# Transposing K as fp32 words, two bf16 tiles per TensorE transpose, in a one-token attention kernel

## The chip, the cores and the metric

The kernel runs on one NeuronCore of a Trainium2 chip. The metric is the device time of one execution in microseconds. Comparisons are always against runs of the kernel before, on the same chip and in the same rounds.

## The reference, cut to what matters

One token attends to a cache of 32768 keys and values. There are 32 query heads and 8 K/V heads of 128 dims, so four query heads share one K/V head.

```python
q = (x @ wq).reshape(B, Sq, Hq, Dh)            # Hq = 32, Dh = 128, Sq = 1
scores = einsum("bhqd,bhkd->bhqk", q, k) * Dh**-0.5   # 8 K/V heads, Sk = 32768
p = softmax(scores); o = einsum("bhqk,bhkd->bhqd", p, v)
a = o.reshape(...) @ wo                         # [4096] @ [4096, 512]
out = g * a + (1 - g) * swiglu(x)               # g: a scalar gate
```

K and V are 67 MB each in bf16, the weights 14 MB. Everything is read once: 148.1 MB.

## The kernel before

Loads go through a ring of five slots of 4 MB. One half of a K head (16384 keys) or of a V head fills one slot; the order is K, V, K, V, and the output weights `wo` come last. The sync engine issues a load when the slot's last reader has signalled.

A matmul contracts over partitions, so K (keys on partitions) has to be transposed before the scores. TensorE does this eight tiles at a time into a PSUM bank, and VectorE (DVE) copies the bank to SBUF as `ktT`. Then come eight score matmuls. One half of a head is 16 such groups, and its V half is 128 more matmuls.

```python
def emit_fill(j, src, q):                       # TPF = 8 tiles of 128 keys
    if j >= NST: pe.wait_ge(sem_cp, j - NST + 1)
    stb = pst[j % NST]                          # a PSUM bank seen as bf16
    for t in range(TPF):
        ins = pe.transpose(stb[:, t*128:(t+1)*128], src[:, q*TPF + t, :], ident[:, :])
    ins.then_inc(sem_fill, 1)

def emit_scores(j):                             # 128 keys x 4 heads each
    ...
    pe.wait_ge(sem_cp, j + 1)
    for t in range(TPF):
        col = (q*TPF + t) * HPG                 # HPG = 4
        ins = pe.matmul(ps_sc[f % NSC][:, col:col+HPG],
                        ktT[:, j % NKT, t*128:(t+1)*128],
                        qT[:, g*HPG:(g+1)*HPG], start=True, stop=True)
    ins.then_inc(sem_sc, 1)

# DVE, once per group:
dve.tensor_copy(ktT[:, j % NKT, :], pst[j % NST]).then_inc(sem_cp, 1)   # 128x1024 bf16

# V: src[:, r, :] is the weight, four columns of exp(scores) stream
ins = pe.matmul(ps_o[:, g*HPG:(g+1)*HPG], src[:, r, :], ET[:, g % NEG, :, k], ...)

# sync engine, the last load, in four pieces (WO_CUT = 16, 8, 4, 4 of 32 rows):
sp.dma_start(wo_v[:, j0:j0+n, :], src[:, j0:j0+n, :]).then_inc(sem_ldo[c], 16)
```

Of the kernel before, what the change touches and what calls it, by code (L numbers as in the profile page):

```python
# [6 lines left out]
ALU = mybir.AluOpType  # L7
AX = mybir.AxisListType
BF16 = mybir.dt.bfloat16
FP32 = mybir.dt.float32  # L10
# [3 lines left out]
def bass_gated_mix__gqa_block_cached__swiglu_ffn__decode_kernel(  # L14
# [14 lines left out]
    G = A_k_cache.shape[1]  # L29
    S = A_k_cache.shape[2]  # L30
    DH = A_k_cache.shape[3]
    H = A_wq.shape[1] // DH
    HPG = H // G
# [15 lines left out]
    TPF = 8  # L49
# [3 lines left out]
    NKT = 8  # L53
    NST = 3
    NSC = 3
# [15 lines left out]
    with ExitStack() as es:  # L71

        def S_(name):
            return es.enter_context(nc.semaphore(name))

        def T(name, shape, dt):
            return es.enter_context(nc.sbuf_tensor(name, shape, dt))
# [8 lines left out]
        sem_ident = S_("s_ident")  # L86
        sem_iota = S_("s_iota")
# [17 lines left out]
        sem_prod = S_("s_prod")  # L105
        sem_gpart = S_("s_gpart")
        sem_qT = S_("s_qT")
        sem_t1 = S_("s_t1")
        sem_tT = S_("s_tT")
        sem_omg = S_("s_omg")  # L110
# [15 lines left out]
        ktT = T("ktT", [128, NKT, TPF * 128], BF16)  # L126
        ET = T("ET", [128, NEG, HPG, NT], BF16)
        ident = T("ident", [128, 128], BF16)
        ones_f = T("ones_f", [128, 128], FP32)
        colidx = T("colidx", [128, 128], FP32)  # L130
        kf = T("kf", [128, 1], FP32)
# [11 lines left out]
        g_col = T("g_col", [128, 1], FP32)  # L143
        omg = T("omg", [128, 1], FP32)
        qT = T("qT", [128, H], BF16)
        sg = T("sg", [128, FC], FP32)
        t1 = T("t1", [128, FC], FP32)
        tT = T("tT", [128, FC], BF16)
# [12 lines left out]
        row = T("row", [OC, 128], BF16)  # L161

        ps = es.enter_context(nc.psum_tensor("ps", [128, 8, 512], FP32))
        pst = [ps[:, i, :].bitcast(BF16) for i in range(NST)]
        ps_e = ps[:, 0, :]
        ps_sc = [ps[:, NST + i, :] for i in range(NSC)]
        ps_o = ps[:, 6, :]
        ps_m = ps[:, 7, :]
# [1 line left out]
        ps_r = ps[:, OC, :]  # L170
        M_X0 = 0
        M_Q0 = M_X0 + 2 * KC
        M_G0 = M_Q0 + H
        M_U0 = M_G0 + FC
        M_B0 = M_U0 + FC
        M_O0 = M_B0 + OC
# [5 lines left out]
        def kv_slot(entry):  # L182
            return slot_of(entry).rearrange("p (r d) -> p r d", r=RH)
# [14 lines left out]
        def load_sem(entry):  # L198
            return sem_ld[place[entry]]

        with nc.Block("main") as block:  # L201

            @block.gpsimd
            def _(pool):
                npool = [0]

                def chain(ins):
                    ins.then_inc(sem_pool, 1)
                    npool[0] += 1
                    pool.wait_ge(sem_pool, npool[0])  # L210

                pool.memset(ones_bf[:, :], 1.0).then_inc(sem_ones, 1)
                pool.memset(ones_f[:, :], 1.0).then_inc(sem_ones, 1)
                chain(pool.memset(ident[:, :], 0.0))
                pool.affine_select(
                    out=ident[:, :],
                    in_=ident[:, :],
                    compare_op=ALU.not_equal,
                    fill=1.0,
                    base=0,  # L220
                    pattern=[[-1, 128]],
                    channel_multiplier=1,
                ).then_inc(sem_ident, 1)
                pool.iota(
                    colidx[:, :],
                    pattern=[[1, 128]],
                    base=0,
                    channel_multiplier=0,
                    allow_small_or_imprecise_dtypes=True,
                ).then_inc(sem_iota, 1)  # L230
                pool.iota(
                    kf[:, :],
                    pattern=[[1, 1]],
                    base=0,
                    channel_multiplier=1,
                    allow_small_or_imprecise_dtypes=True,
                ).then_inc(sem_iota, 1)
                for g in range(G):
                    pool.wait_ge(sem_pmax, 3 * (g + 1))
                    pool.partition_all_reduce(  # L240
                        gmax[:, g, :], pmax[:, g, :], 128, ReduceOp.max
                    ).then_inc(sem_gmax, 1)
# [51 lines left out]
            def _(pe):  # L294
# [19 lines left out]
                def emit_q():  # L314
                    pe.wait_ge(load_sem(("wq",)), 16)
                    for h in range(H):
                        for c in range(KC):
                            ins = pe.matmul(  # L318
                                ps_m[:, M_Q0 + h : M_Q0 + h + 1],
                                wq_v[:, c, h * DH : (h + 1) * DH],  # L320
                                xT[:, c : c + 1],
                                start=(c == 0),
                                stop=(c == KC - 1),
                            )
                    ins.then_inc(sem_pe_q, 1)

                def emit_ffn():
                    pe.wait_ge(load_sem(("F1",)), 32)
                    for base, wt in ((M_G0, wg), (M_U0, wu)):
                        for j in range(FC):  # L330
                            for c in range(KC):
                                ins = pe.matmul(  # L332
                                    ps_m[:, base + j : base + j + 1],
                                    wt[:, c, :].rearrange("d (p j) -> d j p", j=FC)[:, j, :],
                                    xT[:, c : c + 1],
                                    start=(c == 0),
                                    stop=(c == KC - 1),
                                )
                    ins.then_inc(sem_pe_h, 1)
# [15 lines left out]
                def emit_fill(j, src, q):  # L355
                    if j >= NST:
                        pe.wait_ge(sem_cp, j - NST + 1)
                    stb = pst[j % NST]
                    for t in range(TPF):
                        ins = pe.transpose(  # L360
                            stb[:, t * 128 : (t + 1) * 128], src[:, q * TPF + t, :], ident[:, :]
                        )
                    ins.then_inc(sem_fill, 1)

                def emit_scores(j):
                    f, q = j // FPH, j % FPH
                    g = f // 2
                    if j == 0:
                        pe.wait_ge(sem_qT, 1)
                    if q == 0 and f >= NSC:  # L370
                        pe.wait_ge(sem_exp, HPG * (f - NSC + 1))
                    pe.wait_ge(sem_cp, j + 1)
                    for t in range(TPF):
                        col = (q * TPF + t) * HPG
                        ins = pe.matmul(  # L375
                            ps_sc[f % NSC][:, col : col + HPG],
                            ktT[:, j % NKT, t * 128 : (t + 1) * 128],
                            qT[:, g * HPG : (g + 1) * HPG],
                            start=True,
                            stop=True,  # L380
                        )
                    ins.then_inc(sem_sc, 1)

                def emit_pv(g, hf, src, r0, n):
# [11 lines left out]

                emit_x()
                pe.wait_ge(sem_xT, 1)
                pe.wait_ge(sem_ident, 1)
                scored = 0  # L400
                filled = 0
                for e in stream[:-1]:
# [15 lines left out]
                    _, g, hf = e  # L418
                    src = kv_slot(e)
                    pe.wait_ge(sem_exp, 2 * HPG * g + HPG * (hf + 1))  # L420
                    if e == ("V", G - 1, 1):
# [5 lines left out]
                            start=True,  # L427
                            stop=True,
# [23 lines left out]
                for c, n in enumerate(WO_CUT):  # L452
                    pe.wait_ge(sem_ldo[c], 16)
                    for j in range(j0, j0 + n):
                        for oc in range(OC):
                            ins = pe.matmul(  # L456
                                ps_a[:, oc, :],
                                wo_v[:, j, oc * 128 : (oc + 1) * 128],
                                O2[:, j : j + 1],
                                start=(j == 0),  # L460
                                stop=(j == WOJ - 1),
                            )
# [8 lines left out]
            def _(act):  # L471
# [6 lines left out]
                act.wait_ge(sem_pe_h, 1)  # L478
                act.activation(sg[:, :], ps_m[:, M_G0 : M_G0 + FC], ACT.Sigmoid).then_inc(
                    sem_sg, 1  # L480
# [23 lines left out]
            def _(dve):  # L504
                ndc = [0]

                def dchain(ins):
                    ins.then_inc(sem_dchain, 1)
                    ndc[0] += 1
                    dve.wait_ge(sem_dchain, ndc[0])  # L510
# [9 lines left out]
                dve.tensor_reduce(gpart[:, :], prod_col[:, :], AX.X, ALU.add).then_inc(  # L520
                    sem_gpart, 1
                )
                dve.wait_ge(sem_iota, 2)
                for i, thr in enumerate((32.0, 64.0, 96.0)):
                    dchain(dve.tensor_scalar(kq[:, i : i + 1], kf[:, :], thr, None, op0=ALU.is_ge))
                dchain(dve.tensor_tensor(kq[:, 3:4], kq[:, 0:1], kq[:, 1:2], ALU.add))
# [11 lines left out]
                )  # L538
                dve.tensor_copy(pmat[:, :], pmat_f[:, :]).then_inc(sem_pm, 1)
                dve.wait_ge(sem_pe_q, 1)  # L540
                dve.tensor_copy(qT[:, :], ps_m[:, M_Q0 : M_Q0 + H]).then_inc(sem_qT, 1)
                dve.wait_ge(sem_g, 1)
                dve.tensor_scalar(
                    omg[:, :], g_col[:, :], -1.0, 1.0, op0=ALU.mult, op1=ALU.add
# [2 lines left out]
                def emit_t():  # L547
                    dve.wait_ge(sem_sg, 1)
                    dve.tensor_tensor(
                        t1[:, :], sg[:, :], ps_m[:, M_G0 : M_G0 + FC], ALU.mult  # L550
                    ).then_inc(sem_t1, 1)
# [91 lines left out]
```

## Time and profile before

The median was 362.18 us of 3 runs (362.18 to 362.22).

| what | value | view |
|---|---|---|
| span of the profiled run | 360.6 us | page |
| DMA busy, mean rate | 90% or more in nearly all slices, 413 GB/s | page |
| PE, DVE busy | 79%, 52% | page |
| one K half and one V half at the stream's rate | 19.4 us | stretches |
| one group of 8 transposes and 8 scores, warm | 0.65 us | timeline |

The page of the kernel before: busy time by engine, the clock granted to TensorE and the DMA's share in 40 slices (in tenths), the DMA queues, the chain that ended last, and the costliest groups. PE stands for TensorE's matmuls, PEld for its weight loads, DVE for VectorE, ACT for ScalarE and POOL for GpSimd. A group's line gives the source line, engine, operation, output and inputs, shapes and count, then its busy time in us and the mean ns of one, and last the idle time before it with what ended most of it. "issue" is idle time for which the profile shows no releaser.

```profile
PE 283.3 (79%) x6582; PEld 277.6 (77%) x6582; DVE 187.4 (52%) x305; ACT 27.8 (8%) x140; POOL 4.2 (1%) x18
...
PEclk9999678676879696778788796867895885857655
DMA  8999999999999999999999999999999999999972
...
q1 hardware_dynamic: 6200, 148.12, 96.4%
q8 instruction: 51, 0.84, 0.9%
...
PE 66%; issue 25%; DMA 6%; DVE 1%; ACT 0%; POOLq 0%; SPq 0%; POOL 0%; ACTq 0%; DVEq 0%
...
L360 PE MATMUL ps<-ident,ring 128*128 128x128 bf16 x2048 | 187.9, 252 | 21.2 <-issue 13.7
L360 PEld LDWEIGHTS ps<-ident,ring 128*128 128x128 bf16 x2048 | 150.3, 114 | 24.5 <-issue 16.2
L375 PE MATMUL ps<-qT,ktT 128*128 128x4 bf16 x2048 | 90.9, 166 | 9.1 <-issue 7.9
```

Two readings compete here. The DMA line says that the stream never rests. The chain says that the PE is what everything waited for. Two more views separate them. The first is the table by stretches of 19.4 us, where the columns are the length, the busy time of each engine, the granted clock, the DMA share and the rate:

```profile
160.00:179.40 19.40, 15.61 (x364) 15.40 (x362) 11.52 (x18) 3.10 (x17) 0.37 (x1) 0.76 1.01 430
179.40:198.80 19.40, 14.87 (x371) 14.63 (x368) 11.22 (x17) 0.00 (x0) 0.00 (x0) 0.85 1.01 429
```

In each pair of K and V halves the PE is not busy for about 4 us, and the DMA is never idle. The second is the timeline in the middle of a K half (start, length, engine, instruction). "PE L360 x8" starts at 184.52 and again 0.65 us later: that is one group.

```profile
184.52 0.61 PE L360 MATMUL ps<-ident,ring 128*128 128x128 bf16 x8
184.97 0.34 PE L375 MATMUL ps<-qT,ktT 128*128 128x4 bf16 x8
185.17 0.61 PE L360 MATMUL ps<-ident,ring 128*128 128x128 bf16 x8
```

The lengths include the pipeline's latency. What a group costs is read from start to start: 0.445 us from the first transpose to the first score, and 0.20 us for the eight scores. This is 56 ns per transpose and 25 ns per score.

The PE's waits in the kernel before (total, number, longest) mostly have no releaser that the profile shows, hence "issue":

```profile
PE ps L387 <- issue: 29.6, 15, 3.2
PE ps L360 <- issue: 13.7, 11, 2.1
...
PE ps L375 <- issue: 7.9, 10, 1.2
...
PE ps L360 <- DMA ring<-in_A_k_cache_dram: 7.4, 1, 7.4
```

### The profile page before, as it was taken

The numbers are of one execution on the slowest core, as the hardware profiler recorded it, in microseconds if no ns is written. First come the engines' busy times: TensorE is split into PE (matmuls) and PEld (weight loads), VectorE is DVE, ScalarE is ACT, GpSimd is POOL, SyncE is SP. The second block draws the span as 40 slices with busy tenths as digits, with TensorE's granted clock in tenths as the row PEclk, the third lists the DMA queues.
The fourth block names the chain that finished last, engine by engine and source line by source line (L and its number), as shares of the span: only waits on it lengthen the run. The fifth ranks groups of instructions, "written<-read, shape, count | busy, mean of one in ns | idle before, by whom it ended". The sixth has DMA issues, their size and how long they took to land.

```text
span 360.6 us, 14008 instructions
## 1 busy us (share of the span) xinstructions
PE 283.3 (79%) x6582; PEld 277.6 (77%) x6582; DVE 187.4 (52%) x305; ACT 27.8 (8%) x140; POOL 4.2 (1%) x18
## 2 busy tenths in 40 slices
PE   0439998869796897988786969889879778879674
PEld 0439997869696886988685969889779778879674
DVE  0219186637566383737384664638364744728201
ACT  1000004000110003000300012000300030000300
POOL 0000000000000000000000000000000000000000
PEclk9999678676879696778788796867895885857655
DMA  8999999999999999999999999999999999999972
GB/s 346 411 405 449 420 423 448 413 431 433 416 447 416 431 430 427 420 433 427 428 436 409 448 413 434 433 413 453 407 434 432 418 434 429 427 431 412 411 314 88
DMA packets 6260, 148.99 MB, mean 413 GB/s; under 512 B 698, under 2 KB 700, under 8 KB 1212
## 3 DMA queue, kind: packets, MB, share of 16 engines
q1 hardware_dynamic: 6200, 148.12, 96.4%
q8 instruction: 51, 0.84, 0.9%
q14 instruction: 5, 0.04, 0.0%
q10 hardware_dynamic: 4, 0.00, 0.0%
HBM read 148.11 MB, written 0.00 MB: 411 GB/s over the span
## 4 chain that ended last, share of the span: by engine, by line
PE 66%; issue 25%; DMA 6%; DVE 1%; ACT 0%; POOLq 0%; SPq 0%; POOL 0%; ACTq 0%; DVEq 0%
PE ps L360 38%; PE ps L387 13%; PE ps L375 12%; DMA ring<-in_A_k_cache_dram 6%; PE ps L332 2%; PE ps L456 1%; ACT ET L494 0%; DVE ktT L579 0%; PE ps L346 0%; DVE pmaxf L567 0%; PE ps L423 0%; POOLq L201 0%; SPq L250 0%; POOL gmax L240 0%; PE ps L466 0%
## 5 line engine op out<-in xcount | busy, mean ns | idle before, releaser
L579 DVE COPY ktT<-ps 128x1024 bf16<-128x1024 bf16 x256 | 170.7, 692 | 124.0 <-PE ps L360 123.1
L360 PE MATMUL ps<-ident,ring 128*128 128x128 bf16 x2048 | 187.9, 252 | 21.2 <-issue 13.7
L360 PEld LDWEIGHTS ps<-ident,ring 128*128 128x128 bf16 x2048 | 150.3, 114 | 24.5 <-issue 16.2
L375 PE MATMUL ps<-qT,ktT 128*128 128x4 bf16 x2048 | 90.9, 166 | 9.1 <-issue 7.9
L375 PEld LDWEIGHTS ps<-qT,ktT 128*128 128x128 bf16 x2048 | 81.5, 99 | 9.4 <-issue 8.0
L387 PE MATMUL ps<-ET,ring 128*128 128x4 bf16 x2048 | 64.9, 168 | 30.0 <-issue 29.6
L387 PEld LDWEIGHTS ps<-ET,ring 128*128 128x128 bf16 x2048 | 59.8, 101 | 31.3 <-issue 30.8
L494 ACT ACTIVATE ET<-ps,nbias 128x128 bf16<-128x128 f32 x64 | 22.5, 376 | 0.2
L484 ACT ACTIVATE nbias<-gmax 128x4 f32<-128x4 f32 x8 | 1.6, 206 | 270.3 <-POOL gmax L240 270.3
L567 DVE TENSOR_REDUCE pmaxf<-ps 128x4 f32<-128x512 f32 x16 | 11.1, 692 | 12.5 <-PE ps L375 12.5
L494 ACT ACTIVATION_READ_ACCUMULATOR ET<-ps,nbias 128x1 f32 x64 | 13.8, 216 | 0.0
L332 PE MATMUL ps<-xT,ring 128*128 128x1 bf16 x112 | 6.9, 198 | 0.0
L332 PEld LDWEIGHTS ps<-xT,ring 128*128 128x128 bf16 x112 | 6.8, 158 | 0.0
L240 POOL PARTITION_ALL_REDUCE gmax<-pmax x8 | 3.0, 373 | 321.8 <-DVE pmax L571 321.8
L301 PE MATMUL ps<-ones_bf,x_row 1*128 1x1 bf16 x4 | 0.3, 172 | 7.9 <-DMA gw_row<-in_gate_w_dram 7.9
L318 PE MATMUL ps<-xT,ring 128*128 128x1 bf16 x128 | 3.6, 165 | 3.6 <-DMA ring<-in_A_wq_dram 3.6
L318 PEld LDWEIGHTS ps<-xT,ring 128*128 128x128 bf16 x128 | 3.5, 104 | 3.6 <-issue 3.6
L301 PEld LDWEIGHTS ps<-ones_bf,x_row 1*128 1x128 bf16 x4 | 0.2, 114 | 7.9 <-DMA gw_row<-in_gate_w_dram 7.9
L456 PE MATMUL ps<-O,ring 128*128 128x1 bf16 x128 | 3.9, 165 | 1.8 <-issue 1.5
L456 PEld LDWEIGHTS ps<-O,ring 128*128 128x128 bf16 x128 | 3.6, 104 | 2.0 <-issue 1.6
L513 DVE CAST xT<-ps 128x4 bf16<-128x4 f32 x1 | 0.2, 161 | 8.4 <-PE ps L301 8.4
L605 DVE SCALAR_TENSOR_TENSOR res<-ps,g_col,b_pre 128x4 bf16<-128x4 f32 x1 | 0.2, 221 | 5.6 <-PE ps L456 5.6
(48 smaller groups left out, 16.5 us busy)
## 6 DMA issues: line engine op xcount, KB each, us to landing
ring<-in_A_k_cache_dram SPq DMA_DIRECT2D x16, 4096.0 KB, 36.9
ring<-in_A_v_cache_dram SPq DMA_DIRECT2D x15, 4096.0 KB, 33.2
ring<-in_A_wq_dram SPq DMA_DIRECT2D x1, 4096.0 KB, 12.4
ring<-in_A_v_cache_dram SPq DMA_DIRECT2D x1, 2048.0 KB, 27.9
ring<-in_A_wo_dram SPq DMA_DIRECT2D x1, 2048.0 KB, 33.7
ring<-in_B_w_gate_dram SPq DMA_DIRECT2D x1, 1792.0 KB, 26.8
ring<-in_B_w_up_dram SPq DMA_DIRECT2D x1, 1792.0 KB, 30.6
ring<-in_B_w_down_dram SPq DMA_DIRECT2D x1, 1792.0 KB, 43.5
```

What stands on the lines that cost most here:

```text
L240: pool.partition_all_reduce(gmax[:, g, :], pmax[:, g, :], 128, ReduceOp.max).then_inc(sem_gmax, 1)
L301: ins = pe.matmul(ps_m[:, base + c : base + c + 1], srcv[:, c, :], ones_bf[0:1, 0:1], start=True, stop=True,)
L318: ins = pe.matmul(ps_m[:, M_Q0 + h : M_Q0 + h + 1], wq_v[:, c, h * DH : (h + 1) * DH], xT[:, c : c + 1], start=(c == 0), stop=(c == KC - 1),)
L332: ins = pe.matmul(ps_m[:, base + j : base + j + 1], wt[:, c, :].rearrange("d (p j) -> d j p", j=FC)[:, j, :], xT[:, c : c + 1], start=(c = ...
L360: ins = pe.transpose(stb[:, t * 128 : (t + 1) * 128], src[:, q * TPF + t, :], ident[:, :])
L375: ins = pe.matmul(ps_sc[f % NSC][:, col : col + HPG], ktT[:, j % NKT, t * 128 : (t + 1) * 128], qT[:, g * HPG : (g + 1) * HPG], start=True ...
L387: ins = pe.matmul(ps_o[:, g * HPG : (g + 1) * HPG], src[:, r, :], ET[:, g % NEG, :, k], start=(k == 0), stop=(k == NT - 1),)
L456: ins = pe.matmul(ps_a[:, oc, :], wo_v[:, j, oc * 128 : (oc + 1) * 128], O2[:, j : j + 1], start=(j == 0), stop=(j == WOJ - 1),)
L484: act.activation(nbias[:, g, :], gmax[:, g, :], ACT.Copy, scale=-SCALE).then_inc(sem_nbias, 1)
L494: act.activation(ET[:, g % NEG, h, hf * RH : (hf + 1) * RH], sc[:, h, :], ACT.Exp, bias=nbias[:, g, h : h + 1], scale=SCALE, accum_out=esu ...
L567: dve.tensor_reduce(pmaxf[:, f, :], sc, AX.X, ALU.max).then_inc(sem_pmax, 1)
L579: dve.tensor_copy(ktT[:, j % NKT, :], pst[j % NST]).then_inc(sem_cp, 1)
```

## The change

Two neighbouring bf16 tiles of K are, per key, 256 values in a row. Read as fp32 they are 128 words of two values. One fp32 transpose moves the words, so partition k of the result holds dims 2k and 2k+1 of a pair of tiles: the first tile on partitions 0 to 63, the second on 64 to 127. The transposes are halved. The scores must then take the even and the odd dims in two accumulating passes, with weights at a stride of two elements, and with q spread over a block-diagonal operand (`qz`) of two times four columns, one block for each tile. The intent was to relieve the PE.

```diff
     def emit_fill(j, src, q):
-        stb = pst[j % NST]
-        for t in range(TPF):
+        stb = pst_f[j % NST]
+        for t in range(0, TPF, 2):
+            two = src[:, q * TPF + t : q * TPF + t + 2, :].rearrange("p r d -> p (r d)")
             ins = pe.transpose(
-                stb[:, t * 128 : (t + 1) * 128], src[:, q * TPF + t, :], ident[:, :]
+                stb[:, t * 64 : (t + 2) * 64], two.bitcast(FP32), ident_f[:, :]
             )
     ...
-        for t in range(TPF):
+        for t in range(0, TPF, 2):
             col = (q * TPF + t) * HPG
-            ins = pe.matmul(ps_sc[f % NSC][:, col : col + HPG],
-                ktT[:, j % NKT, t * 128 : (t + 1) * 128],
-                qT[:, g * HPG : (g + 1) * HPG], start=True, stop=True)
+            kt = ktT[:, j % NKT, t * 128 : (t + 2) * 128].rearrange("p (k e) -> p e k", e=2)
+            for e in range(2):
+                ins = pe.matmul(ps_sc[f % NSC][:, col : col + 2 * HPG],
+                    kt[:, e, :], qz[:, g, e, :], start=(e == 0), stop=(e == 1))
     ...   # cut: masks sel, an fp32 identity, two q matmuls through sel, four copies into qz
```

The DVE copy is untouched: it moves the same 128x1024 bf16 bits.

More of the change, by code (lines that the diff above doesn't have):

```diff
@@ L107, in bass_gated_mix__gqa_block_cached__swiglu_ffn__decode_kernel @@
         sem_qT = S_("s_qT")
+        sem_sel = S_("s_sel")
+        sem_qz0 = S_("s_qz0")
+        sem_pe_qe = S_("s_pe_qe")
+        sem_qz = S_("s_qz")
         sem_t1 = S_("s_t1")
@@ L145, in bass_gated_mix__gqa_block_cached__swiglu_ffn__decode_kernel @@
         qT = T("qT", [128, H], BF16)
+        ident_f = T("ident_f", [128, 128], FP32)
+        evenidx = T("evenidx", [128, 128], FP32)
+        kf1 = T("kf1", [128, 1], FP32)
+        sel = T("sel", [128, 2, 128], BF16)
+        qz = T("qz", [128, G, 2, 2 * HPG], BF16)
         sg = T("sg", [128, FC], FP32)
@@ L163, in bass_gated_mix__gqa_block_cached__swiglu_ffn__decode_kernel @@
         ps = es.enter_context(nc.psum_tensor("ps", [128, 8, 512], FP32))
+        pst_f = [ps[:, i, :] for i in range(NST)]
         pst = [ps[:, i, :].bitcast(BF16) for i in range(NST)]
@@ L172, in bass_gated_mix__gqa_block_cached__swiglu_ffn__decode_kernel @@
         M_Q0 = M_X0 + 2 * KC
-        M_G0 = M_Q0 + H
+        M_QE = M_Q0 + H
+        M_G0 = M_QE + 2 * H
         M_U0 = M_G0 + FC
@@ L223, in _ @@
                 ).then_inc(sem_ident, 1)
+                chain(pool.memset(ident_f[:, :], 0.0))
+                pool.affine_select(
+                    out=ident_f[:, :],
+                    in_=ident_f[:, :],
+                    compare_op=ALU.not_equal,
+                    fill=1.0,
+                    base=0,
+                    pattern=[[-1, 128]],
+                    channel_multiplier=1,
+                ).then_inc(sem_ident, 1)
+                pool.iota(
+                    evenidx[:, :],
+                    pattern=[[0, 2], [2, 64]],
+                    base=0,
+                    channel_multiplier=0,
+                    allow_small_or_imprecise_dtypes=True,
+                ).then_inc(sem_iota, 1)
+                pool.memset(qz[:, :, :, :], 0.0).then_inc(sem_qz0, 1)
                 pool.iota(
@@ L325, in emit_q @@
                     ins.then_inc(sem_pe_q, 1)
+                    pe.wait_ge(sem_sel, 2)
+                    pe.wait_ge(sem_qT, 1)
+                    for e in range(2):
+                        ins = pe.matmul(
+                            ps_m[:, M_QE + e * H : M_QE + (e + 1) * H],
+                            sel[:, e, :],
+                            qT[:, :],
+                            start=True,
+                            stop=True,
+                        )
+                    ins.then_inc(sem_pe_qe, 1)
                 def emit_ffn():
@@ L357, in emit_fill @@
                         pe.wait_ge(sem_cp, j - NST + 1)
-                    stb = pst[j % NST]
-                    for t in range(TPF):
+                    stb = pst_f[j % NST]
+                    for t in range(0, TPF, 2):
+                        two = src[:, q * TPF + t : q * TPF + t + 2, :].rearrange(
+                            "p r d -> p (r d)"
+                        )
                         ins = pe.transpose(
-                            stb[:, t * 128 : (t + 1) * 128], src[:, q * TPF + t, :], ident[:, :]
+                            stb[:, t * 64 : (t + 2) * 64], two.bitcast(FP32), ident_f[:, :]
                         )
@@ L368, in emit_scores @@
                     if j == 0:
-                        pe.wait_ge(sem_qT, 1)
+                        pe.wait_ge(sem_qz, 4)
                     if q == 0 and f >= NSC:
@@ L372, in emit_scores @@
                     pe.wait_ge(sem_cp, j + 1)
-                    for t in range(TPF):
+                    for t in range(0, TPF, 2):
                         col = (q * TPF + t) * HPG
-                        ins = pe.matmul(
-                            ps_sc[f % NSC][:, col : col + HPG],
-                            ktT[:, j % NKT, t * 128 : (t + 1) * 128],
-                            qT[:, g * HPG : (g + 1) * HPG],
-                            start=True,
-                            stop=True,
-                        )
+                        kt = ktT[:, j % NKT, t * 128 : (t + 2) * 128].rearrange(
+                            "p (k e) -> p e k", e=2
+                        )
+                        for e in range(2):
+                            ins = pe.matmul(
+                                ps_sc[f % NSC][:, col : col + 2 * HPG],
+                                kt[:, e, :],
+                                qz[:, g, e, :],
+                                start=(e == 0),
+                                stop=(e == 1),
+                            )
                     ins.then_inc(sem_sc, 1)
@@ L398, in _ @@
                 pe.wait_ge(sem_xT, 1)
-                pe.wait_ge(sem_ident, 1)
+                pe.wait_ge(sem_ident, 2)
                 scored = 0
@@ L522, in _ @@
                 )
-                dve.wait_ge(sem_iota, 2)
+                dve.wait_ge(sem_iota, 3)
                 for i, thr in enumerate((32.0, 64.0, 96.0)):
@@ L540, in _ @@
                 dve.wait_ge(sem_pe_q, 1)
-                dve.tensor_copy(qT[:, :], ps_m[:, M_Q0 : M_Q0 + H]).then_inc(sem_qT, 1)
+                dchain(dve.tensor_scalar(kf1[:, :], kf[:, :], -1.0, None, op0=ALU.add))
+                for e, k in ((0, kf), (1, kf1)):
+                    dve.tensor_scalar(
+                        sel[:, e, :], evenidx[:, :], k[:, 0:1], None, op0=ALU.is_equal
+                    ).then_inc(sem_sel, 1)
+                dve.tensor_copy(qT[:, :], ps_m[:, M_Q0 : M_Q0 + H]).then_inc(sem_qT, 1)
+                dve.wait_ge(sem_pe_qe, 1)
+                dve.wait_ge(sem_qz0, 1)
+                for e in range(2):
+                    qe = ps_m[:, M_QE + e * H : M_QE + (e + 1) * H].rearrange(
+                        "p (g h) -> p g h", g=G
+                    )
+                    for b in range(2):
+                        dve.tensor_copy(
+                            qz[b * 64 : (b + 1) * 64, :, e, b * HPG : (b + 1) * HPG],
+                            qe[b * 64 : (b + 1) * 64, :, :],
+                        ).then_inc(sem_qz, 1)
                 dve.wait_ge(sem_g, 1)
```

## The prediction

> **What bounds the kernel now.** The DMA queue. The page's slices show it 90% busy or more up to the last two; the table by stretches gives DMA share 1.00 to 1.01 and 425 to 430 GB/s in five consecutive 19.4 us stretches (160 to 257 us), each one K half plus one V half (8.39 MB). The queue's own waits (189 us for transposes to free a K slot, 72 us for a V slot) don't starve it: 33 to 37 us from issue to landing means about four transfers queued. 148.1 MB at 428 GB/s is 346 us; startup and a tail of about 7 us after the last bytes (354 to 360.6) make the span. The chain of waits says PE 66%, issue 25%, but that is the consumer following the stream: per 19.4 us pair the PE is busy 15 to 17 us.
>
> **What the PE needs per pair (timeline).** Eight bf16 transposes take 0.47 us (58 ns each, clock 1.00), eight scores 0.20 us (25 ns each); the group repeats every 0.65 us, which is also the pace of the DVE copies (six in 3.93 us). Sixteen groups are 10.4 us, 128 PV matmuls 3.4 us, gaps named issue 2 to 4 us: 16 to 18 of 19.4 us.
>
> **What the change does.**
> - Halves the transposes to 1024. The built program has one load and one matmul per fp32 transpose, so PE instructions fall by about 15%.
> - Makes each load slower. The Trainium skill ("TensorE: Matmul & The Clock Gate", Weight-path perf modes) says Fast Weight Load is off for fp32. The trace agrees in direction: the row sum's fp32 loads took 311 ns at clock 0.50, a bf16 load about 104. Less a fixed 77 ns (104 minus the 27 ns pace), an fp32 load occupies about 230 ns cold, so 115 ns warm, or half that if transpose mode loads in one pass. Estimate: 55 to 115 ns per fp32 transpose warm, 0.22 to 0.46 us per group against 0.47.
> - Scores stay 2048 matmuls, with eight columns instead of four and weights at a stride of two elements. The strided gate/up weights (14 elements) took 61 ns each, the contiguous q projection 28; at stride two I expect 25 to 35 ns.
> - DVE copies are unchanged: 128x1024 bf16, 692 ns.
> - Startup: masks, two q matmuls and four small copies add about 2 us near 17 to 19 us; the PE waits for K until 24.2 us, so this is hidden.
>
> **On the critical path.** Nearly nothing. The group stays near the DVE's 0.65 us, the pair below 19.4 us, and DMA still sets the time. Less instruction fetch may be worth 0.3 us.
>
> **Prediction: 363 us, range 358 to 392.** Faster by over 2%: 4%; within 2%: 66%; slower by over 2%: 30%.
>
> **What would show each step right.** DMA share near 1.00 in the middle; fp32 transposes pacing at most 115 ns; scores near 25 ns; DVE copies at 0.65 us or a little longer; lower PE busy time.
>
> **What would make it wrong.** (1) The fp32 load is not hidden behind the previous matmul, or takes over 160 ns: the group passes 0.9 us and the pair 19.4 us. (2) The transposes stream half as many columns, so the clock falls to 0.50 in the K phase as it does in the PV phase; with 230 ns loads the group is 1.1 us, the pair 23 us, the time over 400 us. (3) The stride of two halves the speed of the score loads. Any of these makes the PE the bound: DMA share below 0.95, longer queue waits for K slots. Faster by over 2% would need a higher DMA rate, which nothing here provides.

## The result, and the profile after

The changed kernel's median was 361.27 us of 4 runs (361.06 to 361.48), against 362.18 us. The ratio is 0.9975, with a 95% interval of 0.9958 to 0.9992. Ratios here are the mean time of one kernel's fast runs over that of the other's in the same rounds, so not quite the ratio of the medians. A second measurement later gave 0.9968 (0.9946 to 0.9991). The gain is small but real: 0.9 us.

The page of the changed kernel, the same parts as before:

```profile
PE 280.0 (78%) x5560; PEld 273.2 (76%) x5560; DVE 192.2 (54%) x312; ACT 27.8 (8%) x140; POOL 4.9 (1%) x22
...
PEclk9999678969596776959587967869595877879555
DMA  8999999999999999999999999999999999999982
...
q1 hardware_dynamic: 6200, 148.12, 96.6%
q8 instruction: 43, 0.70, 0.8%
...
DMA 63%; PE 32%; SPq 2%; issue 1%; DVE 1%; DVEq 0%
...
L403 PE MATMUL ps<-ident_f,ring 128*128 128x128 f32 x1024 | 184.8, 322 | 40.0 <-DMA ring<-in_A_k_cache_dram 40.0
L403 PEld LDWEIGHTS ps<-ident_f,ring 128*128 128x128 f32 x1024 | 136.2, 165 | 41.3 <-DMA ring<-in_A_k_cache_dram 41.3
...
L422 PE MATMUL ps<-qz,ktT 128*128 128x8 bf16 x2048 | 88.6, 167 | 0.4 <-DVE ktT L642 0.4
```

There are half as many transposes, yet their busy time is nearly the same (184.8 against 187.9 us). In the stretches the DMA's share and rate are as before:

```profile
160.00:179.40 19.40, 15.84 (x319) 15.51 (x318) 11.25 (x18) 3.11 (x17) 0.37 (x1) 0.76 1.00 429
179.40:198.80 19.40, 16.94 (x322) 16.54 (x322) 11.68 (x18) 0.00 (x0) 0.00 (x0) 0.76 1.01 430
```

And so does the group in the timeline: four fp32 transposes take 0.473 us from start to first score (118 ns each), and eight scores again 0.20 us. The group is 0.675 us, 4% longer than before.

```profile
186.62 0.63 PE L403 MATMUL ps<-ident_f,ring 128*128 128x128 f32 x4
187.09 0.34 PE L422 MATMUL ps<-qz,ktT 128*128 128x8 bf16 x8
187.29 0.64 PE L403 MATMUL ps<-ident_f,ring 128*128 128x128 f32 x4
```

One view did change a lot. The PE's waits now name the loads, and little is left under "issue":

```profile
PE ps L403 <- DMA ring<-in_A_k_cache_dram: 40.0, 14, 5.9
PE ps L434 <- issue: 10.8, 8, 1.9
...
PE ps L434 <- DMA ring<-in_A_v_cache_dram: 6.3, 5, 3.8
PE ps L503 <- DMA ring<-in_A_wo_dram: 5.0, 4, 3.6
```

The PE now stands at the head of the stream and waits for it. Before, it ran a few microseconds behind and never waited for a load after the first one. Two questions were therefore put to the chip. Why did half the transposes not make the PE's work smaller? And where do 0.9 us come from if the stream carries the same data?

### The profile page after: what moved, and what is told of

Read it like the earlier page. It is cut to its first block, busy times and chain, and to the rows that moved or that the text cites. A ratio compares the mean times of both kernels' runs of the same rounds, so it can differ in the third digit from the quotient of the medians.

```text
span 359.1 us, 11978 instructions
## 1 busy us (share of the span) xinstructions
PE 280.0 (78%) x5560; PEld 273.2 (76%) x5560; DVE 192.2 (54%) x312; ACT 27.8 (8%) x140; POOL 4.9 (1%) x22
## 4 chain that ended last, share of the span: by engine, by line
DMA 63%; PE 32%; SPq 2%; issue 1%; DVE 1%; DVEq 0%
DMA ring<-in_A_k_cache_dram 53%; PE ps L403 19%; DMA ring<-in_A_wo_dram 10%; PE ps L422 6%; PE ps L434 5%; PE ps L372 2%; SPq L297 2%; DVE ktT L642 0%; PE ps L386 0%; PE ps L503 0%; SPq L279 0%; PE ps L513 0%; DVE row L677 0%; DVE res L668 0%; DVEq L667 0%
## 5 line engine op out<-in xcount | busy, mean ns | idle before, releaser
L642 DVE COPY ktT<-ps 128x1024 bf16<-128x1024 bf16 x256 | 174.1, 692 | 111.9 <-PE ps L403 111.3
L403 PE MATMUL ps<-ident_f,ring 128*128 128x128 f32 x1024 | 184.8, 322 | 40.0 <-DMA ring<-in_A_k_cache_dram 40.0
L403 PEld LDWEIGHTS ps<-ident_f,ring 128*128 128x128 f32 x1024 | 136.2, 165 | 41.3 <-DMA ring<-in_A_k_cache_dram 41.3
L422 PEld LDWEIGHTS ps<-qz,ktT 128*128 128x128 bf16 x2048 | 87.5, 98 | 4.0 <-DVE ktT L642 0.6
L422 PE MATMUL ps<-qz,ktT 128*128 128x8 bf16 x2048 | 88.6, 167 | 0.4 <-DVE ktT L642 0.4
L434 PE MATMUL ps<-ET,ring 128*128 128x4 bf16 x2048 | 64.7, 168 | 17.1 <-issue 10.8
L630 DVE TENSOR_REDUCE pmaxf<-ps 128x4 f32<-128x512 f32 x16 | 11.1, 691 | 11.1 <-PE ps L422 11.1
L541 ACT ACTIVATION_READ_ACCUMULATOR ET<-ps,nbias 128x1 f32 x64 | 13.8, 216 | 0.0
```

What stands on the lines that cost most here:

```text
L403: ins = pe.transpose(stb[:, t * 64 : (t + 2) * 64], two.bitcast(FP32), ident_f[:, :])
L422: ins = pe.matmul(ps_sc[f % NSC][:, col : col + 2 * HPG], kt[:, e, :], qz[:, g, e, :], start=(e == 0), stop=(e == 1),)
L434: ins = pe.matmul(ps_o[:, g * HPG : (g + 1) * HPG], src[:, r, :], ET[:, g % NEG, :, k], start=(k == 0), stop=(k == NT - 1),)
L541: act.activation(ET[:, g % NEG, h, hf * RH : (hf + 1) * RH], sc[:, h, :], ACT.Exp, bias=nbias[:, g, h : h + 1], scale=SCALE, accum_out=esu ...
L630: dve.tensor_reduce(pmaxf[:, f, :], sc, AX.X, ALU.max).then_inc(sem_pmax, 1)
```

## The experiments

A caution first. Several of these kernels compute with stale or incomplete K and V on purpose, and all of them still passed the comparison with the reference. The averaged attention term is evidently too small against the tolerance to show it. So the comparison says nothing about whether the fp32 words arrive bit for bit. What supports that here is only the structure of the change, not a run.

### 1 and 2: take the stream away

From the eleventh ring entry on, each load brings 4 of 128 rows, with the same semaphores. This was done to both kernels.

```diff
+                        elif i >= 2 * NSLOT:
+                            sp.dma_start(dst[:, 0:4, :], src[:, 0:4, :]).then_inc(sem_ld[i], 16)
                         else:
                             sp.dma_start(dst, src).then_inc(sem_ld[i], 16)
```

> The kernel before, but from the eleventh ring entry on each K or V load brings only 4 of its 128 rows per partition (wrong result on purpose), so the stream ends after about 90 us and PE and DVE set the rest. Theory A (the DMA stream bounds the whole kernel, PE and DVE have slack): well under 362 us, about 265 us (90 us of stream, then 11 K halves at 10.4 us and 14 V halves at 3.4 us, and the tail). Rival B (the PE chain bounds the kernel, as the chain of waits with 66% PE suggests): within 5% of 362 us.

> The same cut of the loads in the changed kernel. Theory A with equal transposing cost (one fp32 transpose of 117 ns stands for two bf16 of 58 ns): the same as the run before it within 3%, about 268 us, since the group is 0.675 us against 0.647. Rival C (the change made the K phase cheaper and the DMA stream hides the gain): at least 5% faster than the run before it.

Measured: 304.43 us (ratio 0.8399, 0.8369 to 0.8429) for the kernel before, and 306.59 us (0.8462, 0.8449 to 0.8474) for the changed one. So 58 us go when the stream is taken away. That alone does not settle what bounds the kernel, because most of the PE's gaps without a releaser go with the stream (see below). Run 8 settles it: with 1024 matmuls fewer the kernel before gains 1.3 us, and its PE waits 65.6 us for K loads instead. The expected 265 us was wrong. A pair of halves was summed as 13.8 us. The traces show 15.6 us in the kernel before (the long batches of V matmuls start at 159.15 and 221.48 us, four pairs apart) and 15.8 us in the changed one. The first groups of each K half run at half clock, since the clock falls within the V phase (in run 1 it is 0.83 from 159.2 to 162 us, in a V phase, 0.50 from 162 to 164 and 0.95 from 164 to 168). Without the stream, the margin of the PE against 19.4 us is thus about 4 us, not 6.

The changed kernel is 0.7% *slower* without the stream. So no gain was hidden behind it: rival C falls.

"Issue" in the PE's waits also falls from 52.7 us in the kernel before (four groups) to 10.0 us here:

```profile
PE ps L377 <- issue: 3.6, 4, 1.3
PE ps L389 <- issue: 3.2, 2, 3.0
PE ps L362 <- issue: 3.2, 2, 1.7
```

These gaps belong to a loaded DMA. They fall between matmuls that wait for nothing, in the middle of a batch. The instructions themselves are fetched through the same DMA engines (the row "q8 instruction" on the page), and the packed traces show that the gaps are waits for them: in the kernel before there are 36 such gaps over 0.3 us, 52.5 us in all, and every one ends 1.2 to 1.6 us after a block of instructions has landed. So do the eight in the changed kernel (10.8 us) and the seven of run 1, none of which lies between 93 and 278 us, where the stream is cut. With them the PE before had almost no reserve under the stream, although its own work left 4 us. The change did not make that work smaller, but it has fewer instructions to wait for, which is the likely reason that its PE caught up.

### 3 and 4: take the DVE copy away as well

```diff
-                    dve.tensor_copy(ktT[:, j % NKT, :], pst[j % NST]).then_inc(sem_cp, 1)
+                    w = TPF * 128 if j < NKT else 256
+                    dve.tensor_copy(ktT[:, j % NKT, 0:w], pst[j % NST][:, 0:w]).then_inc(sem_cp, 1)
```

> As the first run, and the DVE copies only 256 of 1024 columns from the ninth copy on (wrong result on purpose), so that the PE alone paces the K phase. If the PE paced the group of 0.65 us already: the same as the first run within 2%. If the DVE copy paced it: faster, and the group below 0.62 us.

> The same in the changed kernel. Equal cost: within 3% of the third run, four fp32 transposes in about 0.47 us and eight scores in 0.20 us. Rival C (gain hidden by the DVE copy's pace): group near 0.43 us, about 38 us less than the third run.

Measured: 303.70 us and 306.51 us, so no change in either kernel. The DVE busy time fell from 185.1 to 94.4 us in the kernel before, and the group stayed. The DVE copy only looked as if it set the pace: it runs at the pace at which the PE fills banks.

### 5: load or stream?

An fp32 transpose of 118 ns could be slow because its weights (the K words) load without the fast path, or because 128 fp32 columns of the identity stream slowly. This run builds on the fourth. It loads 32 of the 128 word columns and streams the same identity.

```diff
+                        w = 128 if j < NST else 32
                         ins = pe.transpose(
-                            stb[:, t * 64 : (t + 2) * 64], two.bitcast(FP32), ident_f[:, :]
+                            stb[0:w, t * 64 : (t + 2) * 64], two.bitcast(FP32)[:, 0:w], ident_f[:, :]
                         )
```

> The changed kernel with PE alone (short loads, short DVE copies), and from the fourth fill on each fp32 transpose loads only 32 of its 128 word columns and still streams the 128 columns of the identity (wrong result on purpose). If the fp32 transpose is paced by streaming 128 fp32 columns at two cycles each: still 117 ns each warm, the group 0.675 us, and about 306 us. If it is paced by loading 128 fp32 columns without the fast load: near 55 ns each, the group about 0.45 us, and about 265 us.

Measured: 299.79 us of 2 runs. The timeline gives the pace:

```profile
181.99 0.60 PE L406 MATMUL ps<-ident_f,ring 128*32 128x128 f32 x4
182.42 0.34 PE L427 MATMUL ps<-qz,ktT 128*128 128x8 bf16 x8
182.62 0.60 PE L406 MATMUL ps<-ident_f,ring 128*32 128x128 f32 x4
```

Four transposes take 0.435 us, or 109 ns each, with a quarter of the load. The load did get shorter (the shortest load record fell from 137 ns in run 4 to 92), yet it costs only the last 9 ns of 118. The rest does not depend on the width of the load. By elimination it is the stream: about twice the 56 ns of a bf16 transpose, for the same 128 columns. No run here shortened the stream itself, so this step is argued and not shown. On this reading each fp32 column takes twice the time, and the change moves the same bytes at the same rate.

### 6 to 9: where 0.9 us come from

Theory F is that fewer instruction bytes pass through the DMA engines. Theory L is that the PE no longer lags at the end. Run 6 is the changed kernel again. Run 7 adds 7000 one-element fills on the idle POOL engine. Runs 8 and 9 leave out every other V matmul, in the kernel before and in the changed one.

```diff
# run 7, POOL, after each group's reduction:
+                    for n in range(1000 if g < G - 1 else 0):
+                        pool.memset(junk[:, 1000 * g + n : 1000 * g + n + 1], 0.0)
# runs 8 and 9:
-                    for r in range(r0, r0 + n):
+                    for r in range(r0 + 1, r0 + n, 2):
```

> The changed kernel, unaltered, for comparison on the same chip: 0.9975 of the kernel before, 361.3 us.

> The changed kernel with 7000 one-element fills added on the idle POOL engine, which nothing waits for: 0.45 MB more of instructions to fetch. Theory F (the 0.9 us gain comes from fewer instruction bytes through the same DMA engines; 0.14 MB at 430 GB/s is 0.33 us): 1.0 to 1.3 us slower than the changed kernel. Theory L (the gain comes from the PE no longer lagging behind the stream at the end): no change within 0.3 us.

> The kernel before with every other PV matmul left out (wrong result on purpose): 1024 matmuls and as many loads less on the PE, 0.13 MB of instructions less, 1.7 us of PE time less per pair. Theory L: the PE catches up with the stream and the time falls to that of the changed kernel, about 361.3 us or a little below. Theory F: 0.3 us less than before, 361.8 us. If the PE were the bound: 16 pairs at 1.7 us less, about 335 us.

> The changed kernel with every other PV matmul left out (wrong result on purpose). Theory L: no change within 0.2 us of the changed kernel, since its PE waits for the stream already. Theory F: 0.3 us less. If the PE were the bound: about 335 us.

Measured: 361.34, 390.80, 360.93 and 359.57 us, with 362.23 us for the kernel before (ratios 0.9968, 1.0775, 0.9959 and 0.9920, each to within 0.3%).

Neither theory had the size right. Run 7 lost 29.5 us where bytes over rate give 1.0. Run 9 gained 1.8 us although its PE waits for the stream already, which contradicts theory L, and although its 0.13 MB less is worth only 0.3 us by theory F.

The page of run 7 shows how. The two lines are the rate in each of its 40 slices (9.7 us each) and the queue that fetched for POOL:

```profile
GB/s 324 431 414 435 444 425 423 426 429 426 429 429 422 426 428 429 426 426 426 425 428 426 428 426 429 429 428 412 426 396 399 432 399 432 319 428 204 60 29 17
...
q14 instruction: 60, 0.49, 0.3%
```

At the end the rate is 29 and 17 GB/s. All sixteen engines together move 427, so one moves 27. One DMA engine works on alone, after the others have finished.

The trace can show this for every run. A full-width load raises its semaphore sixteen times, and the trace has the time of each. Below are the sixteen landings of the last piece of `wo`, sorted, in us from the first instruction, in the profiled run of each kernel. They are read from the trace's record of semaphore increments, so this is not one of the profile's printed views.

```
                 eight earlier                                    eight later
before     346.2 346.3 346.4 346.5 347.6 347.9 348.5 352.0 | 355.4 355.4 355.5 355.6 355.7 355.8 357.0 357.3
changed    346.3 346.4 346.4 346.5 347.0 347.3 347.9 351.0 | 353.9 353.9 354.0 354.4 354.4 354.8 355.8 355.8
run 8      346.1 346.2 346.3 346.4 347.5 348.0 348.2 351.9 | 354.2 354.2 354.3 354.4 354.5 354.5 355.5 355.9
run 9      346.2 346.4 346.6 346.6 347.3 347.4 348.0 351.5 | 352.4 352.4 352.5 352.5 352.6 352.8 354.0 354.1
run 7      359.9 360.1 ... thirteen more, none above 360.5 ...                                       384.8
```

| kernel | PE instruction blocks (q8) | last landing, us | span, us | span less last landing |
|---|---|---|---|---|
| before | 51 | 357.3 | 360.6 | 3.3 |
| changed | 43 | 355.8 | 359.1 | 3.3 |
| run 8 | 43 | 355.9 | 359.2 | 3.3 |
| run 9 | 35 | 354.1 | 357.3 | 3.2 |
| run 7 | 43, and 60 for POOL | 384.8 | 388.0 | 3.2 |

The kernel ends 3.2 to 3.3 us after the last DMA engine delivers the last piece, in all five profiled runs. In the first four, seven engines finish 6 to 11 us earlier, with nothing left to do. This is called theory S below: the late eight engines set the end. The split grows through the kernel: the sixteen landings of the first load lie within 0.6 us (12.5 to 13.1 in the kernel before), those of the tenth such load within 3.2 us, of the twentieth within 6.4 us, of the thirtieth within 9.5 us.

The instruction blocks fit this. A block of 16 KB takes 1.07 us (median of the 43 in the changed kernel). If the PE's blocks fall on eight of the engines, eight blocks less take one from each. The ninth landing in each row, the first of the late group, moves by 1.5 us from before to changed, by 1.2 us from before to run 8, and by 1.5 us from changed to run 9.

The growth within one run shows it more directly. In the kernel before, the loads whose first landing is at 248.8, 258.5, 268.2 and 277.9 us have 35, 36, 38 and 39 blocks fetched by their ninth landing, and 3, 4, 6 and 7 of their landings lie 7.6 us or more behind the first: one landing more for each block. The ninth landing falls back in steps, to 1.5, 2.8, 4.6, 6.1, 7.7 and 9.2 us behind the first, once 5, 15, 24, 32, 41 and 48 blocks have been fetched by then. So a block makes one engine about 1.5 us later, and eight engines take turns. Why it is 1.5 us and not the 1.07 of the block's own record, these runs don't explain.

Runs 8 and 9 lie on the line with the changed kernel: what counts is the number of PE instructions, not whether transposes or V matmuls were left out. The median spans of the timed runs are 360.4 us with 51 blocks, 359.15 and 359.1 with 43 (the changed kernel in run 6, and run 8), and 357.4 with 35. The trace does not give the number of the engine, so that the eight late engines are those that fetch for the PE is inferred from this step by step agreement, and from run 7, where fetching for one more engine made exactly one DMA engine late. No run added instructions to the PE.

A trace of the kernel before has a coincidence: its PE reached the output projection late and ran 111 matmuls without a pause until 357.98 us, so a lag of the PE and the last landing end at the same time. Run 8, which takes the lag away, still ends 3.3 us after its last landing.

### 10 to 12: can the load be shifted to the engines that have time?

The early engines wait 8 us at the end, so moving some of `wo` to them could gain some 3 us, by an estimate from 27 GB/s per engine. The Trainium skill ("DMA: Bandwidth & Descriptors", section Why a DMA increments its semaphore by 16 and not by 1) says that a DMA issued as these are, if it is split over k engines, uses the lowest-numbered k of the sixteen. A load of 8 partitions should then use the lower eight. Which eight are late was not known.

```diff
# run 10 (step = 8 for the pieces in WO_LOW, otherwise 128); pieces 2 and 3
-                            sp.dma_start(wo_v[:, j0 : j0 + n, :], src[:, j0 : j0 + n, :])...
+                            for p in range(0, 128, step):
+                                sp.dma_start(wo_v[p : p + step, j0 : j0 + n, :], src[p : p + step, ...])...
# run 11: every fourth partition of a block of 32, slice(b + q, b + 32, 4)
# run 12: as run 11, WO_CUT = (16, 4, 4, 8), only the last piece, issued last
```

> The changed kernel, same bytes, same result; the second and third piece of the output weights (1.5 MB) are each loaded by sixteen DMAs of 8 partitions instead of one of 128. Theory S (the end is set by eight of the sixteen DMA engines, which carry the PE's instruction blocks and finish the last load 6 to 9 us after the others[...]): if the slow eight are the upper ones, the slow engines give up 96 KB each (about 3.6 us) and the kernel ends near 358 us; if they are the lower ones, near 366 us, in both cases the spread of the sixteen landings of the last load moves accordingly. Rival (the late landings are only an effect of the order of the loads, or the end is set elsewhere): no change within 0.5 us of 361.3.

> As the run before it, but each 8-partition load takes every fourth partition of a block of 32 instead of 8 neighbours, in case neighbours cost rate at the memory (in the run before it, the DMA share between 345 and 355 us was 0.85 to 0.97 at 218 to 239 GB/s, half the usual rate per busy engine). Theory S with the slow eight engines among the upper ones: full rate, the sixteen landings of the last load within about 4 us of each other, and 357.5 to 359 us, faster than both kernels. Theory S with the slow eight among the lower ones: spread over 12 us and about 365 us. If the rate stays at half: about 370 us again, and which engines are slow stays open.

> The two runs before issued their small loads ahead of a load on all engines, and the queue needed 34 us to issue the 34 loads of the output weights, so the last load of all could not land on any engine before about 350 us and the test was confounded. Here only 1 MB goes through sixteen 8-partition loads (every fourth partition), and they are issued last. Theory S with the slow eight among the upper engines: the slow ones give up 64 KB (2.4 us), the others have room for it, and the time is 358.5 to 360.5 us, below both kernels. Slow eight among the lower ones: about 364 to 367 us. A fixed cost of each small load that eats the gain: 361 to 364 us, and the balance cannot be had this way.

Measured: 370.37, 369.51 and 366.36 us (ratios 1.0222, 1.0182 and 1.0101). All three are worse than both kernels. In run 12 the stretches after 345 us (the last three columns are clock, DMA share and rate) show more busy engines than in the changed kernel, which had shares of 0.68 and 0.41 in these stretches, but less data for that:

```profile
345.00:350.00 5.00, 1.38 (x33) 1.10 (x33) 0.59 (x3) 0.00 (x0) 0.00 (x0) 0.50 0.88 272
350.00:355.00 5.00, 1.59 (x60) 1.62 (x61) 0.00 (x0) 0.00 (x0) 0.00 (x0) 0.50 0.54 159
```

The nine packets of 16 KB that started from 348 to 350 us in run 12 took 1227 ns (median), twice the 614 ns of 330 to 335 us. The landings of the small loads go on from 344 to 360.5 us without the gap that one uniform group of eight engines would leave. This suggests, without proving it, that the lower eight include early and late engines. That each small load used eight engines is shown: its semaphore rose nine times, eight times for landings and once for the rest. Which engines are late stays open, and so does whether the balance can be had by other means. No version here beats the changed kernel with a correct result.

## Why the prediction was right

The class, within 2%, was right for the reason given: the stream sets the time. The single value named, 363 us, lay 0.8 us above the kernel before, and the kernel came out 0.9 us below it.

- **The bound.** Right. With the stream cut, 58 us went (run 1); with half the V matmuls cut, 1.3 us (run 8). The chain of waits with 66% PE and 25% issue in the kernel before described an engine that only kept the stream's pace. After the change the same view said DMA 63%.
- **The cost of an fp32 transpose.** The estimate was 55 to 115 ns and it measured 118, so the top of the range was slightly exceeded. The reasoning was wrong in a part: the load was taken for the limit, but with a quarter of it 109 of the 118 ns stayed, which leaves the stream of fp32 columns. That an estimate from the wrong term came so near is luck. The Trainium skill ("TensorE: Matmul & The Clock Gate", Terms) calls transpose mode four times faster for fp32. That may hold against an fp32 matmul, which no run here set beside it, but beside bf16 a transpose of 128 columns took twice as long here (118 against 56 ns).
- **The scores.** Right: 25 ns each at stride two and eight columns, the same as before. The comparison that the estimate leaned on was mixed, though: the strided gate and up weights (61 ns) ran largely at clock 0.50 (from 40 to 43.7 us), the q projection (28 ns) at 1.00.
- **The DVE's pace.** Wrong in its role: 0.65 us was the PE's own pace (run 3). It did no harm to the sum.
- **Startup.** Right: the first transposes started at 24.25 us, against 24.19, and still waited for K.
- **The clock.** The feared fall within the K phase did not come: it was 1.00 from 184.6 to 189.1 us. The mean was 0.773 against 0.777.
- **PE time per pair.** 16 to 18 us was said, gaps included. Without the stream it is 15.6; under the stream the gaps filled nearly all of the 19.4.
- **Instruction fetch.** The mechanism was right and the size was off: 0.3 us was predicted and 0.9 us came. The term was computed as bytes over the rate of all engines. The blocks fall on some engines only, and the slowest engine ends the kernel, so eight blocks cost 1.5 us at the last landing of the profiled runs (and 1.5 us of their spans, 360.6 to 359.1). Over all timed runs of run 6's rounds the median span fell by 1.25 us. The changed kernel spends more time outside its span, 2.11 to 2.26 us in each run against 1.77 to 1.91, and that leaves 0.9 us between the medians. What this extra 0.35 us is was not looked into.

## What to carry to other kernels

Count a packed transpose by the bytes that it streams, not by instructions: two bf16 per fp32 word gained nothing here, because each fp32 transpose took twice the time of a bf16 one. To find the bound, take one resource away and keep the semaphores, and ask what else goes with it, as most of the PE's gaps went with the stream here; the chain of waits names a follower as readily as a leader. When a kernel is bound by DMA, look at the sixteen landings of the last load and not only at the mean rate: instruction blocks make some engines late, and in this kernel fewer instructions were worth three to six times their bytes (0.9 and 1.8 us where the bytes give 0.3).

## What the Trainium skill lacked or had wrong

- "TensorE: Matmul & The Clock Gate" (Terms; Weight-path perf modes) gives no rate for a pass of an fp32 transpose beside bf16. Here it is 109 ns for 128 columns at full clock (118 with a full load of 128 columns), against 56 ns for bf16.
- "Runtime: NRT & Kernel Launch" (Instruction fetch mechanics) calls the cost of crossing a 16 KiB block mostly hidden. In this kernel it is not: a block takes 1.07 us on a DMA engine, PE gaps without a releaser sum to 52.7 us under load against 10.0 us with the stream cut, the 36 over 0.3 us in the kernel before all end 1.2 to 1.6 us after a block lands, and eight blocks fewer moved the ninth landing of the last load by 1.2 to 1.5 us.
- No page says that instruction blocks spread unevenly over the DMA engines. Here the sixteen landings of one load drift apart from 0.6 to 11.1 us, by about 1.5 us on one engine for each block, and 7000 instructions on POOL made one engine 24 us late.
- "DMA: Bandwidth & Descriptors" (Why a DMA increments its semaphore by 16 and not by 1): that a load of 8 partitions runs on eight engines agrees with the nine increments seen in runs 10 to 12. That these are the lowest-numbered could not be checked. That section gives no price for such loads: 1 to 1.5 MB in pieces of 32 or 64 KB cost 5 to 9 us here.
